# Scores, output and state of an attention batch in one TensorE turn, the state in the scores' masked quarter

## The chip, the cores and the metric

The kernel runs on one NeuronCore of a Trainium2 chip. The metric is the device time of one execution in microseconds (us); the figure for a kernel is the median of several runs. The profile and the trace come from one further execution, taken by the hardware profiler. TensorE does matmuls (PE in the rows, its weight loads PEld), VectorE is DVE, ScalarE is ACT, GpSimd is POOL, and SyncE (SP) issues the DMAs.

## The reference

Three stages: a linear attention with decay over 768 steps (4 batches, 8 heads of 48), then two feed-forward networks on the 3072 rows that it gives. The decay attention is computed step by step:

```python
for t in range(S):
    kt, vt, rt = (k[:, :, t], v[:, :, t], r[:, :, t])
    cur = np.einsum('bhd,bhe->bhde', u[None] * kt, vt)
    y[:, :, t] = np.einsum('bhd,bhde->bhe', rt, state + cur)
    state = w[None, :, :, None] * state + np.einsum('bhd,bhe->bhde', kt, vt)
```

```python
x = (silu(x @ w_gate) * (x @ w_val)) @ w_out          # 384 -> 1536 -> 384
h = x @ w_in                                          # 384 -> 2048
x = (h * np.tanh(np.log1p(np.exp(np.minimum(h, 20.0))))) @ w_out
```

## The kernel before

The 768 steps are cut into six blocks j = 0 to 5 of 128 steps, so the fourth block is j = 3; a block with its four batches b is 512 rows for the feed-forward networks. Every feed-forward product runs in split precision: `product` (L246 to L250) issues three matmuls per pair of 128x128 weights, hi times hi, hi weights times the low part, low weights times hi, each with 512 moving columns. Lines L248, L249 and L250 are these three.

A block's attention, per batch, has these parts; each is a function and a word in the step tables:

- `scores` (`at_scores`, L473): for each of the 8 heads k^T r of a block, 128 keys by 128 queries, into two PSUM tiles `at` (one for the even heads g = 0, one for the odd, four heads in a row). The contraction is over 48 features, which lie on partitions 0 to 47 for even heads and 64 to 111 for odd ones.
- `mask` (`at_mask`, L480, VectorE): copies the scores with key before query over the diagonal that GpSimd has put into the SBUF tiles `s0`, `s1` (`diag`, `at_diagonal`, L454).
- `out` (`at_out`, `at_turned`, L522): the output of a batch from the old state and the masked scores, 28 matmuls whose outputs lie in four groups of 32 partitions.
- `state` (`at_state`, L553): k^T v of the block, eight products of 48 by 48, into one PSUM tile, even heads on partitions 0 to 47, odd heads on 64 to 111. `fade` (ScalarE) multiplies the running state with the decay, `sum` (`at_sum`, L569, VectorE) adds the product.
- `hi` and `low` (L589, L599): the output split in two parts as the next network's input; `low` is the last reader of the output's PSUM tile.
- `load` (DMAs of r, k, v of a batch, two SBUF buffers), `first`, `second`, `total` (the bonus, GpSimd L441, L443 and VectorE L449), `later`, `sooner` (the decay on k and r, GpSimd L416, twice), `keys` (GpSimd L463).

A number behind a word means the batch that many places later: "scores1" is the next batch's scores. The matmuls of attention are fp32; each shows as two instructions in the trace.

Attention of blocks 2 to 5 is done beside the first network of the block before. The program is a chain of units, one per (block, 128 hidden features): a gate product, a value product, and the output product of the unit before, 27 matmuls in all. `UNITS` gives the order in a unit; blocks 3 to 5 use "gate fill act val mul tick mine fill out fill tick tick". At each "fill" a `Filler` performs the next step of a table in proportion to the places given: `beside` names, per unit, the steps and the number of places. Blocks 3 to 5 use the table `SPREAD`, once per batch. `tick` advances the loading of weights by one: DMAs, VectorE steps L165, L171, L179, L184, a ScalarE step L200 and a subtraction L206 (on GpSimd for the second network's weights). `mul` is VectorE's L664, and "mine" the low part `g_lo` of the gated product (L672), which the next unit's output product uses. All engines work in program order.

PSUM has eight banks: three accumulators, two buffers `mm` for gate and value products, and three buffers `at` (`ps_at`), which scores, output and state use in turn.

The states of block 1 (its products, L553, and sums) are done at unit 15, one batch per step of `STATES`.

Of the kernel before, what the change touches and what calls it, by code (L numbers as in the profile page):

```python
# [9 lines left out]
F32 = mybir.dt.float32  # L10
F32R = mybir.dt.float32r
U32 = mybir.dt.uint32
AF = mybir.ActivationFunctionType
ALU = mybir.AluOpType
AX = mybir.AxisListType

B, H, S, D = 4, 8, 768, 48
P = 128
CH = 128
NJ = S // CH  # L20
# [5 lines left out]
NPAIR = H // 2  # L26
PD = 64
# [22 lines left out]
    "mask1 total2 later2 sooner2",  # L50
]
SPREAD = [
    "out state load2 diag1", "hi fade keys1", "low", "sum first2", "scores1 second2",
    "mask1", "total2 later2 sooner2",
]

KEYS = [[(1, b, "keys")] for b in range(B)]
STATES = [[(1, b, "state" if i == 0 else "sum")] for b in range(B) for i in range(2)]


AHEAD = [
    [(2, 0, "first second")], [(2, 0, "total later sooner")], [(2, 0, "diag keys")],
    [(2, 1, "first second")], [(2, 1, "total later sooner")],
]
# [14 lines left out]
EARLY = 2  # L79

PAIRED = 7
# [5 lines left out]
def tile_decay_attention_then_two_ffns(  # L87
# [13 lines left out]
    nc = tc.nc  # L101
# [13 lines left out]
    ps_at = ctx.enter_context(tc.tile_pool(name="ps_at", bufs=3, space=PSUM))  # L115
# [161 lines left out]
    at_in = {}  # L277
# [46 lines left out]
    for n in range(B, PRELOAD):  # L324
# [7 lines left out]
        out=mask, in_=mask, pattern=[[1, CH]], compare_op=ALU.is_gt, fill=0.0,  # L332
# [16 lines left out]
    scores = [spool.tile([P, NPAIR, CH], F32, name=f"s{g}") for g in range(2)]  # L349
# [55 lines left out]
    state = const.tile([P, B, NPAIR, 2 * D], F32, name="state")  # L405
    nc.gpsimd.memset(state, 0.0)

    at, bonus = {}, {}
    xs = {}
    HALVES = [slice(late * HALF, (late + 1) * HALF) for late in range(2)]  # L410

# [129 lines left out]
    def at_state(j, b):  # L541
        if j + 1 == NJ:
            return
        a = at_in[j, b]
        if j == 0:
            ps = ps_acc.tile([P, NPAIR, D], F32, name="acc2")
        else:
            ps = ps_at.tile([P, NPAIR, D], F32, name="at")
        for h in range(H):
            i, g = divmod(h, 2)  # L550
            q = slice(g * PD, g * PD + D)
            v = a["v"][:, h, :] if j < EARLY else a["v"][i // 2][:, i % 2, q]
            nc.tensor.matmul(  # L553
                ps[q, i, :], lhsT=a["kn"][:, h, :], rhs=v,
                start=(h < 2), stop=(h >= H - 2), skip_group_check=True,
            )
        a["state"] = ps
        if j == 0:
            at_sum(j, b)

    def at_sum(j, b):
        if j + 1 == NJ:
            return
        ps = at_in[j, b]["state"]
        for i in range(2):
            q = slice(i * PD, i * PD + D)
            old = state[q, b, :, i * D : (i + 1) * D]
            if j:
                nc.vector.tensor_tensor(out=old, in0=ps[q], in1=old, op=ALU.add)  # L569
            else:  # L570
                nc.scalar.activation(old, ps[q], AF.Copy)

    def at_fade(j, b):
        if 0 < j < NJ - 1:
# [31 lines left out]
    def after(j, b, n):  # L606
        n += j * B + b
        return order[n] if n < len(order) else None

    PARTS = {  # L610
        "out": at_out,
        "state": at_state,
        "sum": at_sum,
        "fade": at_fade,
        "hi": at_flip,
# [22 lines left out]
    def at_steps(j, steps):  # L638

        return [[(j, b, step)] for b in range(B) for step in steps]  # L640
# [83 lines left out]
    def at_early(n, what):  # L724
# [6 lines left out]
        out=uw, in0=uw,  # L731
        in1=wt_sb.rearrange("p (n o) -> p n o", o=1).to_broadcast([P, NPAIR, 2]), op=ALU.mult,
# [6 lines left out]
    for n, now in enumerate(early):  # L739
        at_mask(*now)  # L740
        at_mine(*now)
        if n == 0:
            prepare(*early[1])
            at_keys(*early[1])
        if n:
            at_low(*early[n - 1])
        at_early(n + 2, prepare)
        if n + 2 < B:
            at_keys(*early[n + 2])
        at_out(*now)  # L750
        for part in (at_bonus, at_scores) if n else (at_scores, at_bonus):
            at_early(n + 1, part)
        at_y(*now)
        at_fade(*now)
        if now[0] == 0:
            at_state(*now)
        if n == 0:
            warm(4)
        if n + 1 < len(early):
            at_flip(*now)  # L760
        if n >= B - 1:
            weights.tick()

        warm((2, 2, 2, 2, 3, 6, 6, 0)[n])
# [15 lines left out]
    def unit1(n, fill=nothing, tick=nothing):  # L780
# [28 lines left out]
    ready = NF1 + PAIRED  # L809
    beside = {  # L810
        2 * PAIRED: ([k + a for k, a in zip(KEYS, AHEAD[:1] + [[]] * 3)], 3),
        2 * PAIRED + 1: ([STATES[i] + ([] if i % 2 else AHEAD[1 + i // 2]) for i in range(8)], 8),
        ready - 1: (BEGIN + at_steps(2, STEPS), 18),
    }
    beside.update({12 * j - 12: (at_steps(j, SPREAD), 34) for j in range(3, NJ)})
    fill = Filler([], 1)
    due = 0
    for n in range(len(units) - NF1):
# [131 lines left out]
    for n in range(N2 + LAG):  # L950
# [32 lines left out]
        j, f = units2[min(n, N2 - 1)]  # L983
# [86 lines left out]
```

## Time and profile before

| | |
|---|---|
| median of 3 runs | 948.2 us (948.02 to 948.28) |
| profiled execution | 948.35 us |
| its span, first to last instruction | 946.6 us |
| TensorE busy | 938.5 us (99%) |
| VectorE, ScalarE, GpSimd busy | 634.5, 473.3, 176.7 us |
| granted TensorE clock | 1.000 |

A busy time counts matmuls as overlapping records: a matmul's record starts when it starts and its end is modelled, so that two neighbours overlap. The distance from start to start is what a matmul takes of the span. The profile's own line numbers are those of the kernel before.

### The profile page before, as it was taken

The page shows a single profiled execution, that of the slowest core. Times are in us where ns is not written, and L with a number is a line of the kernel's source. Part 1 is how long each engine was busy: PE and PEld are TensorE (multiplying, and loading weights), DVE is VectorE, ACT ScalarE, POOL GpSimd, SP SyncE. Part 2 cuts the span into 40 slices and gives each one's busy share as a digit, 9 for nine tenths or more (in the row PEclk, how much of TensorE's full clock was granted, in tenths as well). Part 3 has the DMA queues.
Part 4 walks back from the last instruction along what each step waited for, and adds up shares of the span by engine and source line. Part 5 has one row for each costly group of instructions (what it writes and reads, how often), then busy time and mean ns, then how long its engine had stood idle before and what let it go on. Part 6 is the DMA issues. An engine that isn't in the chain of part 4 may idle for free.

```text
span 946.6 us, 14850 instructions
## 1 busy us (share of the span) xinstructions
PE 938.5 (99%) x5792; PEld 764.4 (81%) x5792; DVE 634.5 (67%) x1154; ACT 473.3 (50%) x841; POOL 176.7 (19%) x164
## 2 busy tenths in 40 slices
PE   9999999999999999999999999999999999999998
PEld 6778887778888888888888888888888888888886
DVE  8998888545776777532223259878677787687774
ACT  2455443323433443321222157877686777677673
POOL 5100102565564555430000010000000000000000
PEclk9999999999999999999999999999999999999999
DMA  8354632335564866310056641001001010000000
GB/s 318 138 149 135 206 111 69 135 101 168 186 220 156 266 207 203 137 64 1 1 202 198 190 111 33 2 34 34 1 33 34 1 56 12 1 33 1 34 1 33
DMA packets 36213, 95.00 MB, mean 100 GB/s; under 512 B 4272, under 2 KB 4400, under 8 KB 36144
## 3 DMA queue, kind: packets, MB, share of 16 engines
q1 hardware_dynamic: 35712, 93.28, 30.1%
q0 software_dynamic: 432, 0.79, 0.5%
q8 instruction: 45, 0.74, 0.3%
q14 instruction: 24, 0.20, 0.1%
HBM read 71.24 MB, written 22.81 MB: 99 GB/s over the span
## 4 chain that ended last, share of the span: by engine, by line
PE 93%; DVE 3%; DMA 3%; ACT 1%; issue 0%; SPq 0%; DVEq 0%
PE mm L248 13%; PE mm L249 13%; PE mm L250 12%; PE acc L248 12%; PE acc L249 12%; PE acc L250 12%; PE at L249 5%; PE at L250 5%; PE at L248 5%; PE at L522 3%; DMA w_split<-rk_t 2%; PE at L473 2%; PE at L553 1%; DVE w_num L184 1%; DMA w_raw<-w 0%; DVE w_num L165 0%
## 5 line engine op out<-in xcount | busy, mean ns | idle before, releaser
L248 PE MATMUL mm<-x_hi,w_split 128*128 128x512 f32 x546 | 215.8, 395 | 0.0
L249 PE MATMUL mm<-x_lo,w_split 128*128 128x512 f32 x546 | 212.9, 390 | 0.0
L250 PE MATMUL mm<-x_hi,w_split 128*128 128x512 f32 x546 | 212.7, 390 | 0.0
L249 PE MATMUL acc<-g_lo,w_split 128*128 128x512 f32 x483 | 188.6, 391 | 1.1 <-DVE g_lo L672 1.0
L248 PE MATMUL acc<-g_hi,w_split 128*128 128x512 f32 x483 | 189.4, 392 | 0.0
L250 PE MATMUL acc<-g_hi,w_split 128*128 128x512 f32 x483 | 188.2, 390 | 0.0
L664 DVE TENSOR_TENSOR o<-mm,o 128x512 f32<-128x512 f32 x72 | 49.7, 690 | 164.1 <-PE mm L250 130.0
L248 PEld LDWEIGHTS mm<-x_hi,w_split 128*128 128x128 f32 x546 | 102.5, 188 | 23.3 <-issue 0.6
L250 PEld LDWEIGHTS mm<-x_hi,w_split 128*128 128x128 f32 x546 | 102.5, 188 | 21.8
L249 PEld LDWEIGHTS mm<-x_lo,w_split 128*128 128x128 f32 x546 | 102.6, 188 | 20.5
L666 ACT ACTIVATE g_hi<-o 128x512 fp32r<-128x512 f32 x72 | 45.5, 632 | 130.6 <-DVE o L664 130.2
L249 PEld LDWEIGHTS acc<-g_lo,w_split 128*128 128x128 f32 x483 | 90.7, 188 | 21.0 <-DVE g_lo L672 2.2
L248 PEld LDWEIGHTS acc<-g_hi,w_split 128*128 128x128 f32 x483 | 90.7, 188 | 19.8 <-ACT g_hi L666 0.2
L250 PEld LDWEIGHTS acc<-g_hi,w_split 128*128 128x128 f32 x483 | 90.7, 188 | 18.9
L660 ACT ACTIVATE o<-mm 128x512 f32<-128x512 f32 x72 | 42.8, 594 | 100.1 <-PE mm L250 85.8
L897 ACT ACTIVATE e<-h 128x512 f32<-128x512 f32 x96 | 60.1, 626 | 53.4 <-DVE h L891 49.7
L904 ACT ACTIVATE e<-e 128x512 f32<-128x512 f32 x96 | 59.6, 621 | 49.4 <-DVE e L901 49.3
L911 DVE TENSOR_TENSOR h<-h,e 128x512 f32<-128x512 f32 x96 | 60.0, 688 | 20.5 <-ACT e L910 20.5
L249 PE MATMUL at<-x_lo,w_split 128*128 128x512 f32 x174 | 67.7, 389 | 0.0
L250 PE MATMUL at<-x_hi,w_split 128*128 128x512 f32 x174 | 67.7, 389 | 0.0
L248 PE MATMUL at<-x_hi,w_split 128*128 128x512 f32 x174 | 67.7, 389 | 0.0
L672 DVE TENSOR_TENSOR g_lo<-o,g_hi 128x512 fp32r<-128x512 f32 x72 | 53.1, 738 | 21.6 <-ACT g_hi L666 21.6
(105 smaller groups left out, 1332.4 us busy)
## 6 DMA issues: line engine op xcount, KB each, us to landing
w_raw<-w SPq DMA_DIRECT2D x68, 384.0 KB, 3.4
rkv_sb<-rkv_t SPq DMA_DIRECT2D x16, 768.0 KB, 4.9
w2s<-w_raw SPq DMA_DIRECT2D x32, 384.0 KB, 4.0
w_split<-w2s SPq DMA_DIRECT2D x32, 384.0 KB, 3.1
n_sb<-rk_n SPq DMA_DIRECT2D x16, 384.0 KB, 5.7
mid<-o SPq DMA_DIRECT2D x18, 256.0 KB, 2.3
rows<-mid SPq DMA_DIRECT2D x18, 256.0 KB, 2.6
y<-o SPq DMA_DIRECT2D x18, 256.0 KB, 2.3
```

Of the source, the lines that this page charges most:

```text
L248: nc.tensor.matmul(acc, lhsT=wt[:, 0, sl], rhs=hi, start=start, stop=False)
L249: nc.tensor.matmul(acc, lhsT=wt[:, 0, sl], rhs=lo, start=False, stop=False)
L250: nc.tensor.matmul(acc, lhsT=wt[:, 1, sl], rhs=hi, start=False, stop=stop)
L473: nc.tensor.matmul(ps[g][:, i, :], lhsT=a["k"][q, i, :], rhs=a["r"][q, i, :], start=True, stop=True,)
L522: nc.tensor.matmul(ps[q * QUAD : (q + 1) * QUAD, c, :], lhsT=lhsT, rhs=rhs, start=q not in begun_q, stop=ends[q] == n, skip_group_check=True,)
L660: nc.scalar.activation(sg, ps, AF.Silu)
L664: nc.vector.tensor_tensor(out=sg, in0=ps, in1=sg, op=ALU.mult)
L666: nc.scalar.activation(hi, sg, AF.Copy)
L672: eng.tensor_tensor(out=lo, in0=sg, in1=f32(hi), op=ALU.subtract)
L897: nc.scalar.activation(es[n], hs[n], AF.Exp)
L904: nc.scalar.activation(e, e, AF.Ln, bias=1.0)
L911: nc.vector.tensor_tensor(out=hs[n], in0=hs[n], in1=es[n], op=ALU.mult)
```

## The change

Three things are changed. In `SPREAD` the step "scores1" moves to the front of the step with "out" and "state", so that TensorE does the next batch's scores, this batch's output and its state in a row; the GpSimd words first2, second2, later2 and sooner2 come together in one step; one empty step per batch and one at the start of the table are added. From block 3 on the state's eight products go into the two PSUM tiles of the next batch's scores, at partitions 64 to 111 and the first 48 columns of each head's 128: there the key comes after the query, so the mask never reads it. And in block 1 two batches' states share one PSUM tile and one step.

```diff
 SPREAD = [
-    "out state load2 diag1", "hi fade keys1", "low", "sum first2", "scores1 second2",
-    "mask1", "total2 later2 sooner2",
+    "scores1 out state load2 diag1", "hi fade keys1", "low", "sum", "mask1",
+    "first2 second2 later2 sooner2", "total2", "",
 ]
...
-STATES = [[(1, b, "state" if i == 0 else "sum")] for b in range(B) for i in range(2)]
+STATES = [[(1, b + i, what) for i in range(2)] for b in (0, 2) for what in ("state", "sum")]
...
+        begin, end = True, True
         if j == 0:
             ps = ps_acc.tile([P, NPAIR, D], F32, name="acc2")
+        elif j == 1:
+            begin, end = b % 2 == 0, b % 2 == 1
+            if begin:
+                pairs[0] = ps_at.tile([P, 2, NPAIR, D], F32, name="at")
+            ps = pairs[0][:, b % 2]
+        elif j > EARLY:
+
+            nxt = at[after(j, b, 1)]["scores"]
+            a["state"] = [ps[PD : PD + D, :, 0:D] for ps in nxt]
+            for h in range(H):
+                i, g = divmod(h, 2)
+                q = slice(g * PD, g * PD + D)
+                nc.tensor.matmul(
+                    nxt[g][PD : PD + D, i, 0:D], lhsT=a["kn"][:, h, :], rhs=a["v"][i // 2][:, i % 2, q],
+                    start=True, stop=True, skip_group_check=True,
+                )
+            return
         else:
             ps = ps_at.tile([P, NPAIR, D], F32, name="at")
...
-                start=(h < 2), stop=(h >= H - 2), skip_group_check=True,
+                start=begin and h < 2, stop=end and h >= H - 2, skip_group_check=True,
             )
-        a["state"] = ps
+        a["state"] = [ps[g * PD : g * PD + D] for g in range(2)]
...
-        2 * PAIRED + 1: ([STATES[i] + ([] if i % 2 else AHEAD[1 + i // 2]) for i in range(8)], 8),
+        2 * PAIRED + 1: ([s + a for s, a in zip(STATES, AHEAD[1:])], 8),
...
-    beside.update({12 * j - 12: (at_steps(j, SPREAD), 34) for j in range(3, NJ)})
+    beside.update({12 * j - 12: ([[]] + at_steps(j, SPREAD), 34) for j in range(3, NJ)})
```

`at_sum` now takes the two halves from the list `a["state"]`; its sums are the same.

How the instructions stand on TensorE, in block 3. Before, a batch's output (L522) and state (L553) make one turn between FFN products, and some way on the next batch's scores (L473) make another:

```order
L249 MATMUL acc_2635<-g_lo,w_split 128x512
L250 MATMUL acc_2635<-g_hi,w_split 128x512
L522 MATMUL at<-rkv_sb,state 32x128 x12
L522 MATMUL at<-s_231,rkv_sb 32x128 x8
L522 MATMUL at<-s_232,rkv_sb 32x128 x8
L553 MATMUL at<-rkv_sb,n_sb 48x48 x8
L248 MATMUL mm<-x_hi,w_split 128x512
```

```order
L249 MATMUL mm<-x_lo,w_split 128x512
L250 MATMUL mm<-x_hi,w_split 128x512
L473 MATMUL at<-rkv_sb 128x128 x8
L248 MATMUL mm<-x_hi,w_split 128x512
L249 MATMUL mm<-x_lo,w_split 128x512
```

After, the three stand together; the state's new line is L560:

```order
L250 MATMUL acc_2629<-g_hi,w_split 128x512
L473 MATMUL at<-rkv_sb 128x128 x8
L522 MATMUL at<-rkv_sb,state 32x128 x12
L522 MATMUL at<-s_231,rkv_sb 32x128 x8
L522 MATMUL at<-s_232,rkv_sb 32x128 x8
L560 MATMUL at<-rkv_sb,n_sb 48x48 x8
L248 MATMUL mm<-x_hi,w_split 128x512
```

This holds for four batches of block 3, four of block 4 (both with L560) and three of block 5 (scores and output alone).

How they stand on GpSimd, between the diagonals (L454) of two batches of block 3. Before, the subtractions of weights (L206) stand between the multiplies of the bonus (L441, L443) and the decays (L416):

```order
L454 TENSOR_TENSOR s1_232<-ident_213,bonus_2881 128x512
L463 TENSOR_TENSOR n_sb_2737<-n_sb_2737,tabn_256 128x384
L206 TENSOR_TENSOR w_raw_2782<-w_num_2796,w_raw_2782 128x384
L441 TENSOR_TENSOR pr_3022<-n_sb_2961 128x384
L206 TENSOR_TENSOR w_raw_2805<-w_num_2836,w_raw_2805 128x384
L443 TENSOR_TENSOR pr_3022<-pr_3022,u_sb_146 128x384
L206 TENSOR_TENSOR w_raw_2845<-w_num_2900,w_raw_2845 128x384
L416 TENSOR_TENSOR rkv_sb_2960<-rkv_sb_2960,tab_250 128x512 x2
L206 TENSOR_TENSOR w_raw_2909<-w_num_2997,w_raw_2909 128x384
```

After, the four follow one another, with subtractions ahead of them and behind:

```order
L454 TENSOR_TENSOR s1_232<-ident_213,bonus_2879 128x512
L463 TENSOR_TENSOR n_sb_2753<-n_sb_2753,tabn_256 128x384
L206 TENSOR_TENSOR w_raw_2782<-w_num_2802,w_raw_2782 128x384
L206 TENSOR_TENSOR w_raw_2811<-w_num_2840,w_raw_2811 128x384
L206 TENSOR_TENSOR w_raw_2849<-w_num_2896,w_raw_2849 128x384
L441 TENSOR_TENSOR pr_3078<-n_sb_2966 128x384
L443 TENSOR_TENSOR pr_3078<-pr_3078,u_sb_146 128x384
L416 TENSOR_TENSOR rkv_sb_2965<-rkv_sb_2965,tab_250 128x512 x2
L206 TENSOR_TENSOR w_raw_2905<-w_num_3002,w_raw_2905 128x384
```

## Rows read from the trace of the kernel before

**Rows 1.** The page: busy times, granted clock in 40 slices, chain that ended last

```profile
PE 938.5 (99%) x5792; PEld 764.4 (81%) x5792; DVE 634.5 (67%) x1154; ACT 473.3 (50%) x841; POOL 176.7 (19%) x164
...
PEclk9999999999999999999999999999999999999999
...
PE 93%; DVE 3%; DMA 3%; ACT 1%; issue 0%; SPq 0%; DVEq 0%
```

**Rows 2.** Timeline, TensorE, scores turn: start us, duration us, line, names, shapes, count

```profile
246.44 0.39 PE L250 MATMUL mm<-x_hi,w_split 128*128 128x512 f32 x1
...
247.12 0.39 PE L250 MATMUL mm<-x_hi,w_split 128*128 128x512 f32 x1
247.44 1.16 PE L473 MATMUL at<-rkv_sb 48*128 48x128 f32 x16
...
248.87 0.39 PE L249 MATMUL acc<-g_lo,w_split 128*128 128x512 f32 x1
```

**Rows 3.** Timeline, TensorE, a turn of output and state

```profile
256.60 0.39 PE L250 MATMUL acc<-g_hi,w_split 128*128 128x512 f32 x1
...
257.60 1.06 PE L522 MATMUL at<-s,rkv_sb 128*32 128x128 f32 x32
258.58 0.56 PE L553 MATMUL at<-rkv_sb,n_sb 128*48 128x48 f32 x16
...
259.42 0.40 PE L249 MATMUL mm<-x_lo,w_split 128*128 128x512 f32 x1
```

**Rows 4.** Timeline, TensorE, before and after a turn of output alone (block 5)

```profile
391.82 0.39 PE L250 MATMUL mm<-x_hi,w_split 128*128 128x512 f32 x1
...
394.14 0.39 PE L249 MATMUL mm<-x_lo,w_split 128*128 128x512 f32 x1
```

**Rows 5.** Timeline, TensorE, before and after a turn of state alone (block 1)

```profile
138.90 0.39 PE L250 MATMUL mm<-x_hi,w_split 128*128 128x512 f32 x1
...
140.05 0.39 PE L249 MATMUL mm<-x_lo,w_split 128*128 128x512 f32 x1
```

**Rows 6.** Groups by line and shape, the state's matmuls: busy us, mean ns, idle before

```profile
L553 PE MATMUL at<-rkv_sb,n_sb 128*48 128x48 f32 x192 | 6.8, 212 | 0.0
```

**Rows 7.** Timeline, TensorE, FFN output product beside the states of block 1

```profile
148.73 0.39 PE L248 MATMUL acc<-g_hi,w_split 128*128 128x512 f32 x1
150.08 0.50 PE L249 MATMUL acc<-g_lo,w_split 128*128 128x512 f32 x1 [0.96 <-DVE g_lo L672]
```

**Rows 8.** Timeline, VectorE, first and last of the seven steps ahead of that

```profile
142.15 0.69 DVE L664 TENSOR_TENSOR o<-mm,o 128x512 f32<-128x512 f32 x1 [1.59 <-PE mm L250]
...
149.35 0.68 DVE L672 TENSOR_TENSOR g_lo<-o,g_hi 128x512 fp32r<-128x512 f32 x1
```

**Rows 9.** Busy time by stretch: window, its length, PE, PEld, DVE, ACT, POOL, PEclk, DMA

```profile
142.10:150.10 8.00, 7.04 (x45) 5.27 (x43) 7.95 (x8) 1.66 (x4) 6.83 (x6) 1.00 0.30 99
```

**Rows 10.** Timeline, TensorE, the two longer scores turns of blocks 3 to 5

```profile
267.50 1.43 PE L473 MATMUL at<-rkv_sb 48*128 48x128 f32 x16
...
356.22 1.42 PE L473 MATMUL at<-rkv_sb 48*128 48x128 f32 x16
```

**Rows 11.** Timeline, VectorE, beside the first of these

```profile
267.12 0.55 DVE L599 TENSOR_TENSOR x_lo<-at,x_hi 128x384 fp32r<-128x384 f32 x1
```

**Rows 12.** Timeline, GpSimd, first multiply after the turn of rows 3

```profile
265.43 1.22 POOL L441 TENSOR_TENSOR pr<-n_sb 128x384 f32<-128x384 f32 x1 [2.81 <-DMA n_sb<-rk_n]
```

**Rows 13.** Timeline, GpSimd, second multiply and both decays of a batch

```profile
249.14 1.02 POOL L443 TENSOR_TENSOR pr<-pr,u_sb 128x384 f32<-128x384 f32 x1
250.12 2.99 POOL L416 TENSOR_TENSOR rkv_sb<-rkv_sb,tab 128x512 f32<-128x512 f32 x2
```

**Rows 14.** Timeline, VectorE, first and last step of the chain to g_lo beside these

```profile
248.61 0.69 DVE L664 TENSOR_TENSOR o<-mm,o 128x512 f32<-128x512 f32 x1 [0.43 <-ACT o L660]
...
253.71 0.68 DVE L672 TENSOR_TENSOR g_lo<-o,g_hi 128x512 fp32r<-128x512 f32 x1
```

**Rows 15.** Timeline, TensorE, first use of that g_lo

```profile
255.01 0.39 PE L249 MATMUL acc<-g_lo,w_split 128*128 128x512 f32 x1
```

More of the change, by code (lines that the diff above doesn't have):

```diff
@@ L406, in tile_decay_attention_then_two_ffns @@
     nc.gpsimd.memset(state, 0.0)
-    at, bonus = {}, {}
+    at, bonus, pairs = {}, {}, {}
     xs = {}
@@ L563, in at_sum @@
             return
-        ps = at_in[j, b]["state"]
-        for i in range(2):
+        for i, ps in enumerate(at_in[j, b]["state"]):
             q = slice(i * PD, i * PD + D)
@@ L568, in at_sum @@
             if j:
-                nc.vector.tensor_tensor(out=old, in0=ps[q], in1=old, op=ALU.add)
+                nc.vector.tensor_tensor(out=old, in0=ps, in1=old, op=ALU.add)
             else:
-                nc.scalar.activation(old, ps[q], AF.Copy)
+                nc.scalar.activation(old, ps, AF.Copy)
     def at_fade(j, b):
```

## Prediction

> **What bounds the kernel now.** I read the busy table and the chain first [rows 1]: TensorE works 938.5 us of a 946.6 us span, and 93% of the chain that ended last is TensorE. So only TensorE's time and TensorE's waits count; time saved on VectorE or GpSimd counts only where TensorE waits for them. Next I read TensorE's timeline around each kind of attention turn. The FFN products run evenly: three take 0.68 us, 0.227 each [rows 2]. What a turn costs is the distance from the last FFN product before it to the second one after it, less two such periods (0.45). That gives 1.75 - 0.45 = 1.30 us for a turn of scores [rows 2], 2.82 - 0.45 = 2.37 for output with state [rows 3], 2.32 - 0.45 = 1.87 for output alone [rows 4], 1.15 - 0.45 = 0.70 for state alone [rows 5]. The granted clock stays at its upper level of 2.4 GHz in all 40 slices [rows 1], so it plays no part.
>
> **1. Fewer turns.** Output and state in one turn cost 2.37, apart 1.87 + 0.70 = 2.57. Putting two turns together is therefore worth 0.20 us, the way in and out of the FFN stream. The same can be seen from the scores: 0.32 instead of 0.227 to the first product of the turn. The change takes the scores of the next batch into the turn of output and state: four times in block 3, four times in block 4, three times in block 5 (the last batch has no scores after it): 11 x 0.20 = **-2.2 us**.
>
> **2. The state in one column tile.** Before, the eight products of a state alternate between output partitions 0 and 64; now all of them end at partition 64 and above. Does the alternation matter? 16 instructions of the scores, in two row tiles, take 1.16 us with 128 columns each [rows 2]; 32 instructions of the output, in four column tiles and with 128 columns too, take 1.06 [rows 3]. Twice the tiles in turn do twice the work, so tiles overlap, and I take it that one tile has half the rate of two. The 16 state instructions take 0.56 us, of which the last one is 0.212 [rows 3, 6]: 0.35 us of streaming, which becomes 0.70. Eight turns (blocks 3 and 4; block 5 has no state): 8 x 0.35 = **+2.8 us**. Ends: nothing, if the pace of 0.35 belongs to the product and not to the tiles; at most 8 x 0.6 = 4.8, if the 16 took as long as the 16 of the scores, which load 128 weights instead of 48: 1.16 instead of 0.56. I take the doubling, as it comes from the same products. The Trainium skill (TensorE: Matmul & The Clock Gate, "Part 3: Packing small matmuls") has a measured gain of 2.38 for three column tiles, less than threefold; an estimate by that ratio makes two tiles worth 1.6, this term +1.7 and the sum below 1.1 lower. The comparison of rows 2 and 3 has no such loss, so it decides.
>
> **3. States of block 1 in pairs.** Two states in one turn cost 0.70 + 0.35 instead of 2 x 0.70: 0.35 saved for a pair. The first pair brings nothing: behind it TensorE stands still at 148.73, where 1.35 us pass to the next product instead of 0.227 [rows 7], until VectorE's g_lo at 150.03. VectorE's chain to it, 7.88 us long [rows 8], is stretched by GpSimd, busy for 6.83 of 8 us [rows 9], and does not start earlier; what TensorE saves ahead of it, it waits longer. The second pair: **-0.35 us**. (Ends: 0 and -0.7.)
>
> **4. Two late score turns.** Two of the eleven score turns are longer, 1.43 and 1.42 instead of 1.16 [rows 2, 10]: they wait for the second PSUM buffer, which VectorE's x_lo frees (267.12 + 0.55) [rows 11]. In the new order the scores come six places after that step, not two, and a buffer for the state is not asked for any more: 0.27 + 0.26 = **-0.5 us**. What would be late next is the tile of the previous scores, freed by the mask, four places ahead of the turn: some 8 us, with VectorE free to run it.
>
> **5. GpSimd's work in one heap.** load2's two transfers wait for the end of the turn as before; on SP they stand behind one weight transfer more, or one store of mid fewer or more, at four places, which moves no wait, since a new batch is needed some 15 us later. So GpSimd's first multiply starts when n_sb has landed, at 265.43, 6.0 us after 259.42 [rows 3, 12]. Now both multiplies for the bonus and both decays follow one another: 1.22 + 1.02 + 2.99 = 5.2 us [rows 12, 13]. They end 11 us after the turn, and the next turn's scores, which need them, come eight places later; three places make a unit of 27 products, so 8/3 x 27 x 0.227 = 16.3 us. That is covered. Less well covered is VectorE: with three GpSimd instructions beside it, its chain from the gate product to g_lo took 5.78 us (248.61 to 254.39), and TensorE used g_lo at 255.01, 0.62 later [rows 13, 14, 15]. The heap falls on this chain where the turn stands behind the second place of a unit, for batches 0 and 3, in blocks 3 and 4 (block 5 has no weight steps in the chain). Ends for each of the four: nothing, as at 254.39; 1.12, as at 148.73. A fourth GpSimd instruction of 1.0 us takes the 0.62 and some more; I take 0.1 each, near the first end since that row has three of the four: **+0.4 us**.
>
> The mask, the fade, the sum on VectorE (now read from partitions 64 on) and the matmuls' count are the same work off the path, hidden by 8 us and more to the next turn; cost nothing unless VectorE falls behind by that.
>
> **Sum.** -2.2 + 2.8 - 0.35 - 0.5 + 0.4 = +0.15 us against the profiled execution's 948.35, that is 948.5; the median 948.2 lies 0.15 below that execution, so I expect **948.3**, no change. A measurement of this kernel can tell about 0.2% (1.9 us) from no change.
>
> **Rivals.**
> A, faster: the state's eight products do not share their pace with the tile. For it: the start and end of a product are modelled in the records, and no row has two such products in one tile. Against: the comparison under 2. Then term 2 is zero: 948.3 - 2.8 = 945.5.
> B, slower: GpSimd's heap stretches VectorE's chain in every turn that has weight steps. Place: the first g_lo product of an FFN output some 12 us after a turn of blocks 3 and 4. Point: the chain exceeds the 6.4 us from 248.61 to 255.01. A subtraction of weights (L206) follows the heap, so five GpSimd instructions stand in a row, and with 1.0 us for each beyond the three of rows 13 the chain becomes 7.8, the length that cost 1.12 at 148.73. In four turns that is 4.5 - 0.4, so 952.4; in two, 950.1. Against: batches 1 and 2 have their chain before or after the heap, and here there is one VectorE step fewer than at 148.73. The Trainium skill (SBUF — State Buffer, "SBUF: two separate sides") says that VectorE and GpSimd share a pair of ports as an exclusive lock; the stretched chain of rows 8 agrees.
> C, slower: the change doesn't do what it says. Each change of tile shape inside the turn could cost as much as the way back to the FFN products, so that term 1 is zero: 948.3 + 2.2 = 950.5. For it: the Trainium skill (TensorEngine Tiling (Array Packing), "Key Properties") says that a change of tiling mode drains TensorE. Against: the 0.20 of term 1 was found between two such shapes, output and state.
> D, slower: GpSimd is late for the scores, where a weight subtraction ahead of the heap waits for ScalarE. A unit has one or two weight steps; behind the second one the subtraction waits for a chain like that of rows 14, 5.8 us long, that begins some 6 us after the turn. The heap then begins near 12 us and ends near 17, past the 16.3, and TensorE waits up to 1 us in three or four turns: 951 to 952.
>
> **How the numbers follow.** Forecast, no change: 0.54, with a range of its own of 946.4 to 950.1. A 0.17, B 0.17, C 0.06, D 0.06. The range goes down to rival A, 945.4, and up to 951.2, where term 2 is at 3.9 and two or three turns pay the wait of B; beyond are the worst of B and D and a rival A with fuller gains. Faster by over 0.2%: A and some of the forecast's lower edge, 0.20. Slower by over 0.2%: most of B, C and D, and term 2 at its upper end, 0.26. Within: 0.54.
>
> **What would show it.** In the changed profile the turns of blocks 3 and 4 cost 1.30 + 2.37 - 0.20 + 0.35 = 3.82 us by the same reading, those of block 5 1.30 + 1.87 - 0.20 = 2.97; the group of the state's matmuls at the new line lasts some 0.9 us for 16 instead of 0.56. Rival A shows 3.5 and 0.56. The late scores at 1.43 are gone. TensorE's idle before g_lo products stays near 1 us in all; B shows more there, D shows it before scores. The argument is wrong if the time moves by more than 2 us with these turns at 3.8.

## The result and the profile after

The changed kernel takes **958.4 us** (957.4 to 959.2, four runs), against 948.2 for the kernel before in the same session: a ratio of 1.0109, interval 1.0097 to 1.0121. It is 10.2 us slower; I had forecast 948.3, no change, within 945.4 to 951.2. The profiled execution of the changed kernel took 958.87 us, its span is 957.2. In the lines after the change, 17 lines have been added above the evictions: `o` is made at L677 (before L660), `mul`, VectorE's product of gate and value, at L681 (L664), g_hi at L683, g_lo at L689 (L672), the stores of mid, the first network's output, at L715 (L698); the state is L560 in blocks 3 and 4.

The page after, the lines that answer to [rows 1], and the two FFN groups whose idle time has changed (busy us, mean ns, then idle us before them and what ended it):

```profile
PE 940.0 (98%) x5792; PEld 768.1 (80%) x5792; DVE 639.5 (67%) x1154; ACT 473.6 (49%) x841; POOL 180.0 (19%) x164
...
PE 88%; DVE 5%; issue 2%; POOL 2%; ACT 1%; DMA 1%; SPq 0%; POOLq 0%; DVEq 0%; ACTq 0%
...
L248 PE MATMUL mm<-x_hi,w_split 128*128 128x512 f32 x546 | 215.1, 394 | 6.2 <-ACT o L677 6.2
...
L249 PE MATMUL acc<-g_lo,w_split 128*128 128x512 f32 x483 | 188.7, 391 | 3.2 <-DVE g_lo L689 3.1
```

TensorE's busy time has hardly moved, and its share of the last chain fell from 93% to 88%, with GpSimd in it for the first time. So the loss is waiting, and the groups say where: 6.2 us ahead of TensorE's gate product, where there had been none, and 3.1 ahead of g_lo, where there had been 1.0. The waits view of TensorE in blocks 3 to 5 (total us, times, longest) gives the same for that stretch, where the kernel before has no row at all:

```profile
PE mm L248 <- ACT o L677: 6.2, 2, 3.8
PE acc L249 <- DVE g_lo L689: 1.7, 1, 1.7
```

The turns themselves came out as forecast. TensorE's timeline, one merged turn of block 3, then the ends of one of block 5:

```profile
237.10 0.39 PE L250 MATMUL mm<-x_hi,w_split 128*128 128x512 f32 x1
237.42 1.16 PE L473 MATMUL at<-rkv_sb 48*128 48x128 f32 x16
...
240.18 0.92 PE L560 MATMUL at<-rkv_sb,n_sb 128*48 128x48 f32 x16
241.03 0.50 PE L248 MATMUL mm<-x_hi,w_split 128*128 128x512 f32 x1
241.36 0.39 PE L249 MATMUL mm<-x_lo,w_split 128*128 128x512 f32 x1
...
405.15 0.39 PE L250 MATMUL mm<-x_hi,w_split 128*128 128x512 f32 x1
...
408.56 0.40 PE L249 MATMUL acc<-g_lo,w_split 128*128 128x512 f32 x1
```

By the reading of the prediction the first costs 4.26 - 0.45 = 3.81 us (3.82 forecast), the second 3.41 - 0.45 = 2.96 (2.97 forecast); the state's 16 instructions take 0.92 us where they took 0.56 [rows 3].

Both programs have the same 3672 FFN products in the same order, so I compared the start of each with its counterpart. The difference grows to 10.55 us, in these steps:

| where | us |
|---|---|
| new waits of TensorE, at 255.5, 297.8 and 328.8 | 1.90 + 2.56 + 3.93 |
| work at the lower clock behind the last of them: four products 0.80, the turn at 335.8 0.69 | 1.5 |
| merged turns of blocks 3 and 4: 8 x (3.81 - 1.30 - 2.37) | 1.1 |
| merged turns of block 5: 3 x (2.96 - 1.30 - 1.87) | -0.6 |
| two pairs of states, 2 x (1.06 - 1.39), and the g_lo behind the first (1.51 for 1.12) | -0.3 |
| late scores: 0.5 gone [rows 10], 0.2 come (279.5) | -0.3 |
| ahead of the first FFN product | 0.73 |

The last line is no part of the change: in the runs below the first FFN product starts anywhere from 45.0 to 45.7 us, with either turns. The first two lines, **9.9 us**, are what there is to explain.

**The wait at 255.5.** One timeline, by engine: ScalarE, VectorE, GpSimd, TensorE.

```profile
249.48 0.54 ACT L157 ACTIVATE w_num<-w_raw 128x384 f32<-128x384 f32 x1 [1.85 <-DMA w_raw<-w]
249.93 0.51 ACT L200 ACTIVATE w_raw<-w_num 128x384 fp32r<-128x384 f32 x1
250.34 0.58 ACT L677 ACTIVATE o<-mm 128x512 f32<-128x512 f32 x1
...
250.96 0.69 DVE L681 TENSOR_TENSOR o<-mm,o 128x512 f32<-128x512 f32 x1 [1.48 <-ACT o L677]
251.56 1.15 DVE L165 TENSOR_SCALAR w_num<-w_num 128x384 f32<-128x384 f32 x1
...
255.30 1.63 DVE L184 SCALAR_TENSOR_TENSOR w_num<-w_raw,w_num 128x384 uint32<-128x384 uint32 x1
256.85 0.68 DVE L689 TENSOR_TENSOR g_lo<-o,g_hi 128x512 fp32r<-128x512 f32 x1
...
250.51 1.01 POOL L206 TENSOR_TENSOR w_raw<-w_num,w_raw 128x384 fp32r<-128x384 f32 x1 [3.23 <-ACT w_raw L200]
251.49 1.02 POOL L441 TENSOR_TENSOR pr<-n_sb 128x384 f32<-128x384 f32 x1
252.58 1.02 POOL L443 TENSOR_TENSOR pr<-pr,u_sb 128x384 f32<-128x384 f32 x1
253.56 2.95 POOL L416 TENSOR_TENSOR rkv_sb<-rkv_sb,tab 128x512 f32<-128x512 f32 x2
...
255.45 0.39 PE L248 MATMUL acc<-g_hi,w_split 128*128 128x512 f32 x1
257.58 0.50 PE L249 MATMUL acc<-g_lo,w_split 128*128 128x512 f32 x1 [1.74 <-DVE g_lo L689]
```

The heap of GpSimd stands behind a weight subtraction that ScalarE's L200 releases, and ScalarE's next instruction, the eviction L677, releases VectorE's `mul`. So heap and weight step start together. VectorE's four instructions from L165 to L184 take 5.4 us; where GpSimd is idle they take 1.6 (from 244.07 to 245.63 in this trace). But the chain from `mul` to the end of g_lo is 6.57 us (250.96 to 257.53), only 0.79 longer than the 5.78 of [rows 14], while TensorE waits 1.9. The rest is that TensorE is there sooner: 4.7 us after `mul` starts (255.68 if it had not waited), not 6.4 as in [rows 14, 15]. The kernel before, TensorE's first product behind the turn of the same batch (241.03 after), and the landed weights that ScalarE had waited for behind that turn:

```profile
236.97 0.50 PE L248 MATMUL mm<-x_hi,w_split 128*128 128x512 f32 x1
...
245.29 0.55 ACT L157 ACTIVATE w_num<-w_raw 128x384 f32<-128x384 f32 x1 [1.08 <-DMA w_raw<-w]
```

From there to the g_lo product, 18.04 us passed before (255.01): 73 FFN products and the turn of scores at 247.44 [rows 2]. Now 64 products pass and no turn, 241.03 to 255.68, 14.65 us. What starts at the turn's end has not become faster: the weights that ScalarE waits for are in 8.3 us after it before (245.29) and 8.45 after (249.48). 2.0 us went because the turn stands one place (nine products) later, 1.3 because the scores are no longer in between.

**The wait at 328.8**, the first batch of block 4: ScalarE, VectorE, TensorE.

```profile
321.92 0.60 ACT L677 ACTIVATE o<-mm 128x512 f32<-128x512 f32 x1 [2.89 <-DMA mid<-o]
...
331.91 0.52 ACT L200 ACTIVATE w_raw<-w_num 128x384 fp32r<-128x384 f32 x1 [6.20 <-DVE w_num L184]
332.34 0.58 ACT L677 ACTIVATE o<-mm 128x512 f32<-128x512 f32 x1
...
326.11 1.36 DVE L480 COPY_PREDICATED s<-mask,at 128x512 f32<-128x512 uint16 x2
327.36 0.35 DVE L165 TENSOR_SCALAR w_num<-w_num 128x384 f32<-128x384 f32 x1
...
330.27 1.61 DVE L184 SCALAR_TENSOR_TENSOR w_num<-w_raw,w_num 128x384 uint32<-128x384 uint32 x1
...
328.81 0.39 PE L250 MATMUL acc<-g_hi,w_split 128*128 128x512 f32 x1
332.97 0.50 PE L248 MATMUL mm<-x_hi,w_split 128*128 128x512 f32 x1 [3.77 <-ACT o L677]
...
334.50 0.63 PE L250 MATMUL mm<-x_hi,w_split 128*128 128x512 f32 x1
```

Here TensorE waits for a PSUM buffer, which ScalarE's eviction L677 empties. The product to be evicted had ended at 325.1, but the eviction stands behind L200 in ScalarE's program, and L200 waits 6.2 us for the end of VectorE's weight step, the second one of this unit. That step has the heap beside it, and VectorE does the mask (L480) ahead of it. The place at 297.8 has the same chain. Behind the stall the products take 0.43 us each instead of 0.227; the table of stretches (TensorE, weight loads, VectorE, ScalarE, GpSimd, granted clock, DMA share, GB/s) shows the clock at its lower level of 1.2 GHz:

```profile
334.10:336.20 2.10, 2.10 (x6) 1.30 (x4) 2.08 (x5) 1.19 (x3) 0.00 (x0) 0.50 0.00 0
```

The first row of the timeline above, ScalarE at 321.92, is the tail of another collision. The three stores of mid, which free the buffers of `o`, landed in 5.5 us instead of 2.7, as the DMA table has it for 305 to 325 us after and 300 to 318 before (KB each, median us from issue to landing); load2's two transfers had been issued 1.5 us ahead of them, not 7 us:

```profile
mid<-o SPq DMA_DIRECT2D x3, 256.0 KB, 5.5
```

```profile
mid<-o SPq DMA_DIRECT2D x3, 256.0 KB, 2.7
```

**The three places side by side.** The place at 297.8 by engine, VectorE, ScalarE, TensorE, and TensorE's first product behind the turn ahead of 328.8:

```profile
293.70 1.36 DVE L480 COPY_PREDICATED s<-mask,at 128x512 f32<-128x512 uint16 x2
...
299.52 0.52 ACT L200 ACTIVATE w_raw<-w_num 128x384 fp32r<-128x384 f32 x1 [5.87 <-DVE w_num L184]
299.95 0.58 ACT L677 ACTIVATE o<-mm 128x512 f32<-128x512 f32 x1
...
283.61 0.50 PE L248 MATMUL acc<-g_hi,w_split 128*128 128x512 f32 x1
300.58 0.50 PE L248 MATMUL mm<-x_hi,w_split 128*128 128x512 f32 x1 [2.40 <-ACT o L677]
...
314.61 0.50 PE L248 MATMUL acc<-g_hi,w_split 128*128 128x512 f32 x1
```

The kernel before at the places of 297.8 and 328.8: TensorE's first product behind the turn, the eviction, and the gate product that needs its buffer.

```profile
279.43 0.51 PE L248 MATMUL acc<-g_hi,w_split 128*128 128x512 f32 x1
293.17 0.58 ACT L660 ACTIVATE o<-mm 128x512 f32<-128x512 f32 x1
295.20 0.39 PE L248 MATMUL mm<-x_hi,w_split 128*128 128x512 f32 x1
...
305.62 0.50 PE L248 MATMUL mm<-x_hi,w_split 128*128 128x512 f32 x1
321.22 0.58 ACT L660 ACTIVATE o<-mm 128x512 f32<-128x512 f32 x1
325.68 0.51 PE L248 MATMUL mm<-x_hi,w_split 128*128 128x512 f32 x1
```

Counted in us from the first product behind the turn, "asked" is when TensorE would start without waiting, and "ready" is when g_lo (255.5) or the eviction (the other two) ends:

| place | asked, before | asked, after | ready, before | ready, after | ready less asked, after |
|---|---|---|---|---|---|
| 255.5 | 18.04 | 14.65 | 17.42 | 16.50 | 1.85 |
| 297.8 | 15.77 | 14.41 | 14.32 | 16.92 | 2.51 |
| 328.8 | 20.06 | 14.43 | 16.18 | 18.31 | 3.88 |

The last column is each wait but for 0.05 us. Had TensorE asked as late as before, only the place at 297.8 would have waited, 1.15 us. So the shorter distance takes part in all three waits, and at 297.8 the late eviction counts for more: the weight step starts 0.7 us later behind the turn than before, with the mask ahead of it, and beside the heap it takes 4.5 us instead of 2.6 (294.96 to 299.49; before, 290.10 to 292.70). At 328.8 it takes 4.5 instead of 2.4.

So four things come together: GpSimd's heap, the loads behind the turn, VectorE's mask ahead of a weight step, and less work of TensorE between the turn and the late step. The experiments take the first three apart.

### The profile page after: what moved, and what is told of

It reads as the page before. It is cut to its first block, busy times and chain, and to the rows that moved or that the text cites. A ratio compares the mean times of both kernels' runs of the same rounds, so it can differ in the third digit from the quotient of the medians.

```text
span 957.2 us, 14830 instructions
## 1 busy us (share of the span) xinstructions
PE 940.0 (98%) x5792; PEld 768.1 (80%) x5792; DVE 639.5 (67%) x1154; ACT 473.6 (49%) x841; POOL 180.0 (19%) x164
## 4 chain that ended last, share of the span: by engine, by line
PE 88%; DVE 5%; issue 2%; POOL 2%; ACT 1%; DMA 1%; SPq 0%; POOLq 0%; DVEq 0%; ACTq 0%
PE mm L248 11%; PE mm L250 11%; PE mm L249 11%; PE acc L249 11%; PE acc L248 11%; PE acc L250 11%; PE at L249 5%; PE at L250 4%; PE at L248 4%; PE at L522 3%; PE at L473 2%; DVE w_num L184 1%; DVE w_num L171 1%; PE at L499 1%; PE mm L473 1%
## 5 line engine op out<-in xcount | busy, mean ns | idle before, releaser
L681 DVE TENSOR_TENSOR o<-mm,o 128x512 f32<-128x512 f32 x72 | 49.7, 690 | 159.8 <-PE mm L250 119.1
L683 ACT ACTIVATE g_hi<-o 128x512 fp32r<-128x512 f32 x72 | 45.5, 632 | 131.7 <-DVE o L681 131.4
L677 ACT ACTIVATE o<-mm 128x512 f32<-128x512 f32 x72 | 42.7, 593 | 98.6 <-PE mm L250 82.7
L689 DVE TENSOR_TENSOR g_lo<-o,g_hi 128x512 fp32r<-128x512 f32 x72 | 54.3, 753 | 21.6 <-ACT g_hi L683 21.6
```

What stands on the lines that cost most here:

```text
L677: nc.scalar.activation(sg, ps, AF.Silu)
L681: nc.vector.tensor_tensor(out=sg, in0=ps, in1=sg, op=ALU.mult)
L683: nc.scalar.activation(hi, sg, AF.Copy)
L689: eng.tensor_tensor(out=lo, in0=sg, in1=f32(hi), op=ALU.subtract)
```

## The experiments

Times are medians; each ratio is to the kernel before in the same session (947.9 to 948.4).

**heap_apart**: the heap is undone; the mask comes one place later with it.

```diff
-    "scores1 out state load2 diag1", "hi fade keys1", "low", "sum", "mask1",
-    "first2 second2 later2 sooner2", "total2", "",
+    "scores1 out state load2 diag1", "hi fade keys1", "low", "sum first2", "second2",
+    "mask1", "total2 later2 sooner2", "",
```

> The changed kernel (958.4 us) with GpSimd's heap taken apart: the two bonus multiplies in the places of sum and behind it, the two decays two places later, as before the change; turns, transfers and state untouched. Theory H (GpSimd's four multiplies in a row run beside VectorE's weight step, which ends late; ScalarE's next eviction or g_lo stands behind it): the waits at 255.5 (1.9 us) and 297.8 (2.6) go, that at 328.8 (3.9, and 0.8 at the lower clock behind it) falls below 1.5: 950 to 951.5. Theory L (the loads issued behind the turn delay the stores of mid at a block's start, and ScalarE's eviction waits for them): the wait at 328.8 stays above 3: 954 to 956. Theory P (the new places put state sum and mask just ahead of a weight step): all three stay, 957 to 959.

951.05 us, ratio 1.0030 (1.0019 to 1.0041). The waits at 297.8 and 328.8 are gone; for g_lo TensorE waits 0.84 near 255 and 0.44 near 302. H holds: by the two ratios 7.5 of the 10.2 us hang on the heap. Two scores turns are now later (1.36 and 0.43 us), the longer one behind the mask that moved one place back.

**load_later**: only load2 moves, two places later.

```diff
-    "scores1 out state load2 diag1", "hi fade keys1", "low", "sum", "mask1",
+    "scores1 out state diag1", "hi fade keys1", "low load2", "sum", "mask1",
```

> The changed kernel with the loads of the batch after next (load2) issued two places, some 4 us, later; all else untouched. Theory L: the stores of mid at the block's start land in 2.7 us instead of 5.5, ScalarE's eviction no longer waits 2.9 us for them, and the wait at 328.8 with its slow clock goes: 953 to 954. Theories H and P: the wait at 328.8 falls by under 1 us, the others stay: 957 to 959; if the loads come too late for GpSimd's first multiply, slower than 959.

955.67 us, ratio 1.0079 (1.0064 to 1.0094). ScalarE waits for no store of mid any more; TensorE's wait at 328 falls from 3.93 to 2.56, that for g_lo from 1.90 to 0.76, that near 297 stays at 2.56. The time lies between the two ranges that I had given. So L is a part, some 2.8 us, and not where I had looked for all of it.

**shift_one**: `[[], []] + at_steps(j, SPREAD)`, one empty step more.

> The changed kernel with every step of blocks 3 to 5 one place (a third of a unit, 2 us) later; the order within a turn is untouched. Theory H: the heap still follows a weight step in half of the batches, so waits move but their sum stays within 2 us: 956 to 960. Theory P (the places alone decide): the sum of the three waits changes by more than 4 us, up or down: under 954 or over 962. Theory L: the block's first turn moves away from the stores of mid or onto them: the wait near 328 changes by 2 us or more, the others by less.

957.38 us, ratio 1.0096 (1.0079 to 1.0113). The waits have moved (2.11 at 277.5, 1.12 at 303.5, 2.57 at 351.1, late scores of 1.16 at 281.9) and come to 7.0 us, with smaller ones to some 8, as H expected. The places of mask and sum alone (P) do not decide.

**single_states**: `STATES` and its PSUM tile as before the change.

> The changed kernel with the states of block 1 one to a turn and a bank again, as before the change. Turns then cost 4 x 0.70 instead of 1.06 + 1.06 us, +0.66; the wait for g_lo behind the first state falls from 1.5 to 1.1, -0.4. All three theories: 958.4 + 0.3 = 958.7, and the waits of blocks 3 and 4 stay. If the pairs set something that lasts (the 0.7 us by which the changed kernel is late ahead of its first FFN product, or the phase of the weight transfers), the time falls by over 1 us.

958.74 us, ratio 1.0110 (1.0095 to 1.0125), as expected. The wait for g_lo behind the first state is 1.13 again.

**heap_before**: the heap, put into the kernel before.

```diff
-    "out state load2 diag1", "hi fade keys1", "low", "sum first2", "scores1 second2",
-    "mask1", "total2 later2 sooner2",
+    "total1 out state load2 diag1", "hi fade keys1", "low", "sum", "scores1",
+    "mask1", "first2 second2 later2 sooner2",
...
```

> The kernel before (948.4 us) with its turns, states and transfers as they are, and only GpSimd's heap made: the two bonus multiplies put ahead of the two decays in the last place of a batch in blocks 3 to 5, VectorE's sum of the bonus one place later. Theory H: the heap alone brings waits of TensorE for g_lo or for ScalarE's eviction, of 1 to 2.5 us in two or three places: 950.5 to 953. Theory M (it takes the merged turn: TensorE's long turn, with load2 and the mask and sum behind it, brings the lateness, and the heap only lengthens it): no wait over 1 us in blocks 3 and 4, 948 to 949.

948.12 us, ratio 1.0000 (0.9991 to 1.0009). This is against H as I had it: the heap alone, in this place, costs nothing. VectorE's timeline at the same unit, and TensorE's use of that g_lo:

```profile
248.34 1.14 DVE L165 TENSOR_SCALAR w_num<-w_num 128x384 f32<-128x384 f32 x1
...
252.06 1.65 DVE L184 SCALAR_TENSOR_TENSOR w_num<-w_raw,w_num 128x384 uint32<-128x384 uint32 x1
253.62 0.68 DVE L672 TENSOR_TENSOR g_lo<-o,g_hi 128x512 fp32r<-128x512 f32 x1
...
254.94 0.39 PE L249 MATMUL acc<-g_lo,w_split 128*128 128x512 f32 x1
```

The weight step is as long as in the changed kernel (5.37 us, 248.34 to 253.71; there 251.56 to 256.93), and g_lo is still done 0.64 us before TensorE asks. What differs is when the step starts, and how far TensorE is by then. That made the next theory, S: what the merged turn takes away is the time that a turn of TensorE had given to the others.

**heap_bare**: the same heap in the kernel before, in the place of the scores, so that no turn follows it closely.

```diff
-    "out state load2 diag1", "hi fade keys1", "low", "sum first2", "scores1 second2",
-    "mask1", "total2 later2 sooner2",
+    "out state load2 diag1", "hi fade keys1", "low", "sum",
+    "scores1 first2 second2 later2 sooner2", "mask1", "total2",
```

> The kernel before with GpSimd's heap made in the place of the scores instead of the last one of a batch: from there 7.4 us pass to the next turn of TensorE, where the run heap_before (948.1) had the turn of output and state some 2.5 us behind the heap. Turns, states, loads as before. Theory S: what cost nothing with a turn behind it costs now, in the units that hold two weight steps: waits of 0.5 to 2 us in two to four places of blocks 3 and 4, 949.5 to 952. Theory M: it takes the merged turn, so no wait over 0.5 us in blocks 3 and 4: 948 to 948.6.

949.17 us, ratio 1.0011 (1.0002 to 1.0021). One new wait appears, of 1.09 us, again for ScalarE's eviction:

```profile
273.82 0.50 PE L248 MATMUL mm<-x_hi,w_split 128*128 128x512 f32 x1 [0.93 <-ACT o L660]
```

It shows that a heap can make TensorE wait without any merged turn. But it is one place, not two to four, and the time is below S's range as well as above M's: a weak hit for S.

**one_step**: the changed kernel with fewer weight steps to a unit.

```diff
-        due += 2 if n < 2 * PAIRED else 1 if n < ready else 0 if n < 24 else 1.3
+        due += 2 if n < 2 * PAIRED else 1 if n < ready else 0 if n < 24 else 1.04
```

> The changed kernel (958.4 us) with 1.04 weight steps to a unit of blocks 3 to 5 in place of 1.3, so that hardly any unit has two; the last ones end in block 5. Turns, heap and loads as the change has them. Theory S (the merged turn leaves units of 27 products, 6.1 us, with no turn of TensorE in them; where such a unit holds two weight steps and the heap, VectorE and ScalarE need longer than TensorE, which waits; before, a turn of 1.3 or 2.4 us fell into nearly every unit and covered it): with one weight step to a unit they fit but for some tenths, the waits of 1.9, 2.6 and 3.9 us fall below 1 each: 950 to 952. Theory M (the merged turn alone makes them late, by mask, sum and loads behind it): waits fall by less than half, 954 to 957.

948.98 us, ratio 1.0011 (1.0002 to 1.0020): by the two ratios 9.3 us come back, more than expected, with the merged turns, the heap and the loads as the change has them. Of TensorE's waits in blocks 3 to 5 only the first row is left, while ScalarE, up to 400 us, still waits for the stores of mid:

```profile
PE acc L249 <- DVE g_lo L689: 0.2, 1, 0.2
```

```profile
ACT o L677 <- DMA mid<-o: 4.7, 2, 2.4
```

**one_step_before**: the same edit in the kernel before.

> The kernel before with 1.04 weight steps to a unit in place of 1.3, to stand beside the run one_step (949.0). Theory S: with its turns spread the kernel before has no wait of this kind to lose, only the two late scores turns (0.27 and 0.26): 947.5 to 948.2. If fewer steps to a unit help by themselves, whatever the turns: 946 to 947.3.

948.04 us, ratio 0.9998 (0.9989 to 1.0008). Fewer steps to a unit are worth nothing with the turns of before. Together with heap_before this shows the form of the cause: with the turns of before the second weight step costs 0, and the heap 0 or, in the place of heap_bare, 1.0; taken out of the changed kernel, the one gives back 9.3 us and the other 7.5.

**heap_spread**: "sum first2", "mask1 second2", "later2", "sooner2 total2": no two multiplies in one place.

> The changed kernel with GpSimd's four multiplies in four places, at most one of them in each (first with sum, second with mask, then each decay), and the mask as early as the change has it. Theory H: chains of VectorE stay under 4 us, the late scores of the run heap_apart (1.4 and 0.4 us, behind the mask one place later) go too, its waits for g_lo (0.84 and 0.44) stay or shrink: 949 to 950. Theory P (places decide, not the heap): it may be as slow as 955 or more.

951.05 us, ratio 1.0030 (1.0018 to 1.0042), a miss. No scores turn is late, but two waits for ScalarE's eviction are left (1.35 and 1.15) and one for g_lo (0.96), with ScalarE waiting 5.0 us for stores of mid and 4.1 for weights. The mask stands ahead of the weight step again: at the places of 297.8 and 328.8 the eviction starts 15.1 and 15.0 us behind the turn, where heap_apart, with the mask behind that step, has 13.6 and 13.1, and TensorE asks after 14.4 in both. So the mask's place, theory P, has a part as well.

**split_load**: heap_apart, and the larger one of load2's transfers two places later.

```diff
-    "scores1 out state load2 diag1", "hi fade keys1", "low", "sum first2", "second2",
+    "scores1 out state natural2 diag1", "hi fade keys1", "low both2", "sum first2", "second2",
```

> The run heap_apart (951.05 us) with the larger one of the two loads behind the turn (768 KB of 1152) issued two places later. Theory L as a part beside H: ScalarE's waits for the stores of mid (4.6 us in two) and for weights (2.8) shrink by half or more, and the waits of TensorE at 254.6 (0.84) and 301.5 (0.44) with them: 949.5 to 950.3. If the transfers cost TensorE nothing once the heap is apart: 951 within 0.5.

949.37 us, ratio 1.0015 (1.0006 to 1.0024). ScalarE's wait for mid is gone (4.6 us before this edit), TensorE's 0.44 and the second late scores with it: 1.4 us for the loads by the two ratios. A wait for g_lo of 0.74 and late scores of 0.94 stay; the time is just under the expected range.

**all_apart**: split_load with the mask in the place that the change gave it ("mask1 second2").

> The changed kernel's turns and pairs with the heap apart, the larger load two places later and the mask where the change has it, that is the run split_load (949.4 us) with the mask one place earlier. What should be left are the terms of the turns: state in one tile 8 x 0.35, merging 11 x -0.20, pairs -0.66 + 0.38, no late scores -0.5, and one wait for g_lo of 0.7: +0.5 us on 948.0, so 948.5, with the late scores of split_load (0.94) gone. If the mask one place earlier puts VectorE's chain late again: 949.5 or more.

949.43 us, ratio 1.0010 (1.0000 to 1.0020), a miss by 0.9 of the 948.5. The late scores of 277.7 are gone, and a scores turn at 326.4 is 0.72 late instead, waiting for GpSimd's decays. The mask's earlier place costs the eviction 1.1 us (13.4 behind the turn at both places, 12.3 and 12.2 in split_load), which TensorE's 14.4 still covers. I found no order in which the merged turns of blocks 3 and 4 pay.

**last_and_pair**: the kernel before, with the change's table for block 5 alone and one pair of states, that of batches 2 and 3.

```diff
+LAST = [
+    "scores1 out state load2 diag1", "hi fade keys1", "low", "sum", "mask1",
+    "first2 second2 later2 sooner2", "total2", "",
+]
...
+STATES += [[(1, 2, "state"), (1, 3, "state")], [], [(1, 2, "sum"), (1, 3, "sum")], []]
...
+    beside[12 * NJ - 24] = ([[]] + at_steps(NJ - 1, LAST), 34)
```

> The kernel before with two parts of the change alone: merged turns in block 5, where there is no state (3 x -0.20 us), and the states of the last two batches of block 1 in one turn (-0.34). If turn costs add up where nobody else is late: 948.4 - 0.9 = 947.5, and a ratio of 0.9990. If the heap of block 5 makes TensorE wait as well: 948.4 or more.

**946.76 us**, ratio 0.9986 (0.9978 to 0.9995): 0.14% faster than the kernel before, with an interval that leaves out 1. Its three merged turns cost 2.96 each and its pair 1.06, and TensorE has no new wait. Of the 1.2 us the turns account for 0.94; the late scores of [rows 10] are absent in its profile too, so the rest may be those.

## Why the prediction was wrong

1. **Fewer turns, -0.20 each: right.** Block 5 shows it bare, 2.96 against 1.30 + 1.87. Rival C, for which I had cited the Trainium skill (TensorEngine Tiling (Array Packing), "Key Properties": a change of tiling mode drains TensorE), falls: three shapes in one turn cost their bodies and one way in and out; nothing beyond shows in the 2.96.
2. **The state in one column tile, +0.35 each: right.** 3.81 is 1.30 + 2.37 - 0.20 + 0.34, and 0.92 for 16 instructions was forecast as 0.9. Rival A falls. The ratio of 2.38 for three tiles from the Trainium skill (TensorE: Matmul & The Clock Gate, "Part 3: Packing small matmuls"), by which I had estimated about 0.2 for a turn, does not fit these eight products; the doubling does.
3. **Pairs of states: right.** The second pair saved 0.33, the first lost its gain to the wait for g_lo (1.12 to 1.51, and back in single_states).
4. **Late scores, -0.5: right but for 0.2.** The two of [rows 10] went. The turn at 279.5 starts 0.22 late, when the second decay has ended (279.95); the longer scores at 335.8 are the lower clock.
5. **GpSimd's heap on VectorE's chain, +0.4: this is the step that failed.** In its place stand 8.4 us of waits and 1.5 us at the lower clock. I wrote that VectorE's chain had 0.62 us to spare, since TensorE used g_lo at 255.01, and priced a fourth multiply against that 0.62. That spare time was a distance on TensorE's side, and the change shortened it: the scores turn that term 1 merged took 1.3 to 1.4 us out of it at each of the three places, and the turns' later places another 2.0 at 255.5 and 4.3 at 328.8. I counted the 0.20 that a merged turn saves on the path and not the 1.4 to 5.6 us of cover that moved away from these places. At the two evictions the late step also ends 2.6 and 2.1 us later behind the turn, beside the heap and with the mask ahead of it, which I had called hidden. With the turns of before neither the heap (heap_before) nor the second weight step (one_step_before) costs anything.

The term looked for its waits behind batches 0 and 3. Two of these four places waited, batch 3 of block 3 (297.8) and batch 0 of block 4 (328.8), for the eviction; the wait for g_lo came behind batch 1 of block 3, which the term had left out.

In the same term I held that load2's new place on SP "moves no wait". It moved two: the stores of mid (2.7 to 5.5 us) and, by the shorter distance, the weights; load_later and split_load put that at 1.4 to 2.8 us.

**Rival B** named heap, weight step and g_lo, and the wait at 255.5 is of its kind; its price of 1.12 came from the wait at 148.73, where the cover does not change, and it looked for g_lo alone. Two of the three waits, 6.5 of 8.4 us, were on the other way out of the same lateness, ScalarE's queue: eviction behind L200 behind VectorE. I had listed who waits for VectorE's chain and left out ScalarE. **Rival D** is there with 0.2 us, at 279.5, not with 1. The clock, which I had set aside since it stood at 2.4 GHz in all slices, took another 1.5 us behind the longest wait.

That the parts do not add up (7.5 for the heap, 9.3 for the second weight step and up to 2.8 for the loads, for a loss of 10.2) fits the table of the three places: a wait needs a late step and a short distance, and without the heap or the second step most late steps end within what TensorE leaves. That heap and second step cost this much only with the changed turns is shown by heap_apart, one_step and their controls. That the lost distance is the reason on the side of the turns rests on the table; the mask, which the change put ahead of the weight step, has a part in it (1.1 us of the eviction, all_apart against split_load). Merging and moving were not taken apart: neither merged turns at the old distances nor unmerged turns in the new places were run.

## What to carry to other kernels

A turn of TensorE on other work is cover for every engine behind it: when turns are merged or moved, measure again, for each late step, the distance from what starts it to the TensorE instruction that needs it, and subtract what has left that stretch; spare time read from the old trace does not carry over. Follow a late VectorE also into ScalarE's queue, where an eviction can stand behind a conversion that waits for it. Ask the same of each step that is moved, here the mask: what now stands behind it. And try a change's parts one by one: here two of them gained 1.2 us where the whole lost 10.2.

## What was not expected of the hardware

A weight step of VectorE takes 1.6 us alone and 5.4 beside GpSimd's heap; L179 in it, with one SBUF input, 0.35 and 1.44. That agrees with the exclusive lock of the Trainium skill (SBUF — State Buffer, "SBUF: two separate sides"), by which one engine waits for a whole instruction of the other: each of the four became 0.8 to 1.1 us longer, and one of GpSimd's takes 1.0. For an instruction with one SBUF input the page wants a two-port mode, which no row here shows. Unexpected was that so long a step costs nothing by itself: it stood in a kernel of 948.1 us and in one of 958.4.

The clock did not follow the length of a wait alone. In the profiled execution of the changed kernel no product is slow behind the 2.56 us at 297.8 (granted clock 1.00 from 297 to 304 us); in that of load_later, waits of 2.56 us at 295.7 and 328.3 were followed by 13 products at 0.43 us, the lower level (0.58 on average from 300 to 304 us).
